# V of later batches by casting DMA, recalibrated plan constants, and q and k of two batches through the DMA crossbar

## The chip, the cores and the metric

One core of a Trainium2 chip runs the whole program. The metric is device microseconds (us) of one execution. The kernel before: 208.59 us, the median of three runs (207.99 to 209.14). "Span" is the time from the first to the last instruction of the profiled execution, some 2 us less than the run time. "Clock" is the mean granted TensorE clock, 1.0 being full. The names of engines are those of the profile: PE (matmul), PEld (weight load), DVE (vector), ACT (scalar), POOL (GpSimd), SP (sync, which only issues DMAs here).

## The reference, cut to what matters

```python
B, H, S, D = 4, 8, 768, 64              # q, k, v: float32, 0.1 * randn
# attention: heads 0, 2, 6 causal over everything; the other five see 4 sink keys and a window of 64
a = softmax(mask(q @ k.T / sqrt(D)));  x = (a @ v) as (B, S, 512)
# wave MLP
theta = x @ w_theta
zr, zi = x * cos(theta), x * sin(theta)
u = x + w_tok_r @ zr + w_tok_i @ zi     # mixes over the 768 tokens
out = u + maximum(u @ w_ch, 0)
```

## The kernel before: the parts that matter here

The kernel doesn't issue instructions in program order. It describes steps, each with the engines that may take it, an assumed duration and the steps it must follow, and a list scheduler fixes, at build time, the order of every engine. At run time each engine works strictly through its list; semaphores only make it wait. Batches are counted 1 to 4 in this text, 0 to 3 in the code.

```python
# q, k: casting loads from the POOL queue, then 12 PE transposes into a PSUM bank, then one copy
# that also puts the tokens in order
def turn_qk(what, b, n):
    pt = state["pt", what, n] = mine_bf()
    for j in range(NB):
        for x, h in enumerate(PAIRS[n]):
            nc.tensor.transpose(pt[64 * x:64 * x + 64, j * 128:(j + 1) * 128], state[what, b][:, h, j * D:(j + 1) * D], ident)

def keep_qk(what, n):
    dst = (qT if what == "q" else kT)[n]
    copy(dst.rearrange("d (p j) -> d p j", j=NB), state.pop(("pt", what, n))[:, :S].rearrange("d (j p) -> d p j", j=NB))

# V: float32 loads from the SP queue, a cast on DVE or POOL, and for the five window heads a copy
# shifted by 64 tokens
def load_v(b, n, after=None): ...
    for x, h in enumerate(PAIRS[n]):
        nc.sync.dma_start(out=t[:, x], in_=src[:, h])
def cast_v(b, n): copy(vt[:, h0:h1 + 1:2, :, :D], state["v", b, n])
def shift_v(b, n, x):
    copy(vx[:64, s], vt[:64, h]); copy(vx[64:, s, 1:], vt[64:, h, :NB - 1])

# x of batches 2 to 4 and most u are already transposed by DMA, from the SP queue
def send_x(b, i): ... nc.sync.dma_start_transpose(...)
# ... (cuts: scores, exponentials, values, theta, waves zr and zi, mix, channel, stores, the scheduler)
```

The softmax here doesn't subtract the row's maximum and nothing guards it: scores larger than these inputs give would overflow.

## Time and profile before

| | before |
|---|---|
| run time, median of 3 | 208.59 us |
| span, clock | 206.3 us, 0.998 |
| PE busy; PE idle | 179.0 us; 27.3 us |
| q of batch 2 lands | 41.3 us |
| values of batch 3 start; theta of batch 4 starts; end | 116.8; 167.4; 206.3 us |

### The profile page before, as it was taken

What the parts mean: (1) busy time and instruction counts of PE and PEld (TensorE: products, weight loads), DVE (VectorE), ACT (ScalarE), POOL (GpSimd) and SP (SyncE); (2) the same over time, 40 slices, a digit from 0 to 9 for tenths busy, and PEclk for the clock granted to TensorE, in tenths of its full rate; (3) what the DMA queues carried; (4) which work ended last, traced back from release to release, by engine and by line L of the source; (5) the groups of instructions that cost most, each with busy time, mean ns of one, the idle gap of its engine ahead of it and who ended that gap; (6) DMA issues with size and microseconds to landing.
All of it is one profiled execution on the core that took longest, in us unless ns stands there. A gap on an engine that the chain in (4) does not pass through costs nothing.

```text
span 206.3 us, 4846 instructions
## 1 busy us (share of the span) xinstructions
PE 179.0 (87%) x1988; PEld 99.4 (48%) x1988; DVE 134.2 (65%) x236; ACT 108.7 (53%) x135; POOL 76.1 (37%) x140
## 2 busy tenths in 40 slices
PE   0689599667999999999999999989699999597992
PEld 0436388444546584454653557534335664242440
DVE  7336966389984574799855287499917446944442
ACT  2397914789885735550677464696683427300010
POOL 8966960394752000674123200099350002900000
PEclk9999999999999999999999999999999999999999
DMA  5998999999999995952223047784223254113404
GB/s 169 182 222 168 157 199 196 192 202 208 206 204 204 115 126 134 232 144 102 54 81 126 4 78 130 185 180 96 49 81 102 79 102 105 55 47 76 153 25 152
DMA packets 58252, 27.45 MB, mean 133 GB/s; under 512 B 44408, under 2 KB 55160, under 8 KB 58232
## 3 DMA queue, kind: packets, MB, share of 16 engines
q1 hardware_dynamic: 47704, 17.85, 40.6%
q0 software_dynamic: 10528, 9.31, 28.3%
q8 instruction: 15, 0.25, 0.6%
q14 instruction: 5, 0.04, 0.1%
HBM read 25.71 MB, written 6.29 MB: 155 GB/s over the span
## 4 chain that ended last, share of the span: by engine, by line
PE 64%; DVE 14%; DMA 13%; ACT 4%; POOL 2%; issue 1%; DVEq 0%; POOLq 0%
PE bank L502 28%; PE bank L525 9%; DMA qb<-in_q_dram 8%; PE pair L366 7%; DVE zr L243 7%; PE pair L453 7%; PE pair L479 6%; PE bank L300 5%; DMA kb<-in_k_dram 3%; DVE zi L243 2%; DVE qT L240 1%; DMA uT<-u 1%; DVE vx L240 1%; PE bank L545 1%; DMA out_dram<-ot 1%
## 5 line engine op out<-in xcount | busy, mean ns | idle before, releaser
L502 PE MATMUL bank<-zr,wtokTr 128*128 128x512 bf16 x144 | 38.6, 380 | 4.3 <-DVE zr L243 3.4
L502 PE MATMUL bank<-zi,wtokTi 128*128 128x512 bf16 x144 | 38.3, 379 | 0.2 <-DVE zi L243 0.2
L366 PE MATMUL pair<-qT,kT 64*64 64x128 bf16 (+5 forms) x380 | 26.7, 262 | 5.1 <-ACT P L385 2.1
L506 DVE TENSOR_TENSOR u<-x,bank 128x512 bf16<-128x512 bf16 x24 | 16.3, 684 | 18.6 <-PE bank L502 18.5
L525 PE MATMUL bank<-w_ch_sb,uT 128*128 128x512 bf16 x96 | 24.1, 380 | 1.9 <-DMA uT<-u 1.5
L247 POOL TENSOR_SCALAR_AFFINE_SELECT P<-P 128x256 bf16<-128x256 bf16 (+1 forms) x48 | 18.2, 398 | 20.1 <-ACT P L385 11.0
L243 POOL TENSOR_TENSOR zi<-x,st 128x512 bf16<-128x512 bf16 x11 | 14.7, 1350 | 29.0 <-ACT st L486 28.9
L529 DVE SCALAR_TENSOR_TENSOR ot<-bank,u 128x512 f32<-128x512 f32 x24 | 16.5, 689 | 13.5 <-PE bank L525 13.2
L243 DVE TENSOR_TENSOR zr<-x,ct 128x512 bf16<-128x512 bf16 x24 | 22.9, 992 | 1.5 <-ACT ct L484 1.5
L366 PEld LDWEIGHTS <-kT 64*64 64x64 bf16 (+1 forms) x380 | 13.0, 111 | 22.4 <-issue 19.5
L385 ACT ACTIVATE P<-pair 128x1024 bf16<-128x1024 f32 (+2 forms) x24 | 21.8, 922 | 3.0 <-PE pair L366 2.8
L479 PE MATMUL pair<-w_theta_sb,xT 128*128 128x512 bf16 x96 | 22.8, 379 | 0.3 <-ACT st L486 0.2
L502 PEld LDWEIGHTS <-wtokTi 128*128 128x128 bf16 x144 | 13.5, 98 | 17.3 <-issue 2.1
L502 PEld LDWEIGHTS <-wtokTr 128*128 128x128 bf16 x144 | 12.6, 98 | 18.9 <-issue 6.5
L382 ACT ACTIVATE P_st<-pair 128x512 bf16<-128x512 f32 (+1 forms) x16 | 12.8, 813 | 12.9 <-PE pair L366 12.8
L240 ACT COPY uT<-bank 128x512 bf16<-128x512 bf16 x5 | 2.9, 585 | 29.3 <-PE bank L515 29.3
L240 POOL CAST vt<-st_v 128x768 bf16<-128x768 f32 x9 | 10.3, 1167 | 20.7 <-DMA st_v<-in_v_dram 20.6
L484 ACT ACTIVATE ct<-pair,half_pi 128x1024 f32<-128x1024 f32 x12 | 13.1, 1118 | 8.0 <-PE pair L479 5.1
L460 DVE TENSOR_TENSOR x<-pair,r 128x512 bf16<-128x512 f32 x24 | 16.6, 691 | 0.8
L453 PE MATMUL pair<-vx,P_st 128*128 128x65 bf16 x120 | 16.0, 200 | 0.3 <-DVE P_st L402 0.3
L300 PE MATMUL bank<-ident,kb 128*64 128x128 bf16 x192 | 8.9, 244 | 8.4 <-DVE kb L240 5.2
L453 PE MATMUL pair<-vt,P_st 128*128 128x65 bf16 x120 | 16.0, 200 | 0.0
(77 smaller groups left out, 291.6 us busy)
## 6 DMA issues: line engine op xcount, KB each, us to landing
st_v<-in_v_dram SPq DMA_DIRECT2D x32, 192.0 KB
out_dram<-ot SPq DMA_DIRECT2D x24, 256.0 KB
qb<-in_q_dram POOLq DMA_DIRECT2D x3, 768.0 KB, 16.8
kb<-in_k_dram POOLq DMA_DIRECT2D x3, 768.0 KB, 19.6
wtok<-in_moe_w_tok_r_dram POOLq DMA_DIRECT2D x3, 384.0 KB, 15.4
wtok<-in_moe_w_tok_i_dram POOLq DMA_DIRECT2D x3, 384.0 KB, 16.6
w_theta_sb<-in_moe_w_theta_dram POOLq DMA_DIRECT2D x1, 512.0 KB, 9.5
w_ch_sb<-in_moe_w_ch_dram POOLq DMA_DIRECT2D x1, 512.0 KB, 24.3
```

The lines of the kernel that those rows point to most:

```text
L240: {"ACT": nc.scalar.copy, "DVE": nc.vector.tensor_copy, "POOL": nc.gpsimd.tensor_copy}[state["step"].eng](o, i)
L243: {"DVE": nc.vector, "POOL": nc.gpsimd}[state["step"].eng].tensor_tensor(o, a, b, ALU.mult)
L247: nc.gpsimd.affine_select(out=t, in_=t, compare_op=ALU.is_ge, fill=0.0, base=base, pattern=pattern, channel_multiplier=cm)
L300: nc.tensor.transpose(pt[64 * x:64 * x + 64, j * 128:(j + 1) * 128], state[what, b][:, h, j * D:(j + 1) * D], ident)
L366: nc.tensor.matmul(ps[half, yy, c:c + w], l, r, start=True, stop=True, skip_group_check=True)
L385: nc.scalar.activation(P.rearrange("p (y c) -> p y c", y=2), ps[:, :, :w0], AF.Exp, scale=scale)
L453: nc.tensor.matmul(o, l, r, start=(m == 0), stop=True, skip_group_check=True)
L460: nc.vector.tensor_tensor(dst, av[:, :, :, :D], r.unsqueeze(3).to_broadcast([128, 2, 4, D]), ALU.mult)
L479: nc.tensor.matmul(ps[:, y], state["xT", b][:, kk, (i + y) * 128:(i + y + 1) * 128], w_theta_sb[:, kk], start=(kk == 0), stop=(kk == KD - 1))
L502: nc.tensor.matmul(py, wtokT[n][:, s, t * 128:(t + 1) * 128], z[:, s], start=(g == 0 and m == 0), stop=(g == 2 and m == 3))
L525: nc.tensor.matmul(pc, uT[:, kk], w_ch_sb[:, kk], start=(kk == 0), stop=(kk == KD - 1))
L529: nc.vector.scalar_tensor_tensor(ot, state.pop(("pc", b, t)), 0.0, state.pop(("u", b, t)), ALU.max, ALU.add)
```

## The change

Its intent is to take work off engines that the end waits for. V of batches 2 to 4 is cast by the DMA that loads it and shifted by four DMA moves in SBUF, so DVE and POOL lose the casts and shifts. q and k of batches 3 and 4 no longer go through PE: DVE puts the two heads of a pair side by side (`qp`), the DMA crossbar transposes, and a copy on DVE, ACT or POOL orders the tokens. The durations that the scheduler assumes are set anew. To make room, q and k have one buffer each instead of two. The core of the diff:

```diff
-                    ns += 0.7 * max(0, min(ns, free[other] - t))
+                    ns += max(0, free[other] - t) if e == "DVE" else 0.3 * max(0, free[other] - t)
@@ buffers (the transposes land in the four wtok buffers)
+        "qp": (8, [128, NB, 2, D], BF16),
         "wtok": (4, [128, 2, S], BF16),
@@ V
+    def fetch_v(b, half):
+        heads = slice(4 * half, 4 * half + 4)
+        nc.gpsimd.dma_start(out=vts[b % 2][:, heads, :, :D], in_=v[b].rearrange("h (j p) d -> p h j d", p=128)[:, heads])
+    def move_v(b):
+        for s, h in ((slice(0, 1), slice(4, 5)), (slice(1, 5), slice(1, 8, 2))):
+            nc.sync.dma_start(out=x[:64, s], in_=t[:64, h])
+            nc.sync.dma_start(out=x[64:, s, 1:], in_=t[64:, h, :NB - 1])
@@ q, k
+    def pair_qk(what, b, n):
+        nc.vector.tensor_copy(t, state[what, b][:, h0:h1 + 1:2].rearrange("p x (j d) -> p j x d", d=D))
+    def send_qk(what, n):
+        nc.sync.dma_start_transpose(t, state.pop(("qp", what, n)).rearrange("p j x d -> p (j x d)"))
@@ turn_steps
+                if b > 1:
+                    pair = paired[what, b, n] = add("DVE", 350, ...pair_qk..., take="qp", port=True)
+                    tp = add("SP", 1250, ...send_qk..., [pair], take="wtok")
+                    land = add("DMAH", 600, None, [tp], give=[pair])
+                    kept[what, b, n] = add({"DVE": 960, "ACT": 1550, "POOL": 1520}, 0, ...keep_qk..., [land] + old, give=[tp], port=True)
+                    continue
@@ assumed durations (the rest alike)
-    gate = [add("DMA", ns, None) for ns in (3500, 6500)]
+    gate = [add("DMA", ns, None) for ns in (6500, 5000)]
-                    shift[b, h] = add({"DVE": 340, "POOL": 960}, ...
+                    shift[b, h] = add({"DVE": 510, "POOL": 1000}, ...
```

More of the change, by code (lines that the diff above doesn't have):

```diff
@@ L204 @@
     kS = [None] + [big.tile([128, 32], BF16, name=f"kS{n}") for n in (1, 2, 3)]
-    vt = big.tile([128, H, NB, D + 1], BF16, name="vt")
-    vx = big.tile([128, len(STREAM), NB, D + 1], BF16, name="vx")
+    vts = [big.tile([128, H, NB, D + 1], BF16, name="vt0")]
+    vxs = [big.tile([128, len(STREAM), NB, D + 1], BF16, name="vx0")]
+    v_room = big.tile([128, 4, 2, NB, D], F32, name="v_room")
+    room = v_room.rearrange("p n x j d -> p (n x j d)").bitcast(BF16)
+    e0, e1 = H * NB * (D + 1), len(STREAM) * NB * (D + 1)
+    vts.append(room[:, :e0].rearrange("p (h j c) -> p h j c", h=H, j=NB))
+    vxs.append(room[:, e0:e0 + e1].rearrange("p (s j c) -> p s j c", s=len(STREAM), j=NB))
     vs = big.tile([128, B, len(STREAM), D + 1], BF16, name="vs")
@@ L223 @@
         "st": (2, [128, 2, DM], F32),
+        "qp": (8, [128, NB, 2, D], BF16),
         "wtok": (4, [128, 2, S], BF16),
-        "st_v": (4, [128, 2, NB, D], F32),
     }
     buffers = {name: [(psum if name in ("pair", "bank") else big).tile(shape, dt, name=f"{name}{i}") for i in range(n)] for name, (n, shape, dt) in SLOTS.items()}
+    SLOTS["st_v"] = (4, None, None)
+    buffers["st_v"] = [v_room[:, n] for n in range(4)]
     state = {}
@@ L251, in load_qk @@
     def load_qk(what, b, heads):
-        if (what, b) not in state:
-            state[what, b] = two.tile([128, H, NB * D], BF16, tag=f"{what}b", name=f"{what}b")
+        state[what, b] = state[what, 0]
         src = {"q": q, "k": k}[what][b].rearrange("h (p j) d -> p h (j d)", p=128)
@@ L263, in cast_first, with load_v, cast_v, shift_v @@
         copy(state[what, 0][:, 0:3:2], state.pop(("first", what)))
-    def load_v(b, n, after=None):
-        src = v[b].rearrange("h (j p) d -> p h j d", p=128)
-        t = state["v", b, n] = mine()
-        if after is not None:
-            nc.vector.tensor_copy(t[:, :, 0, 0], after[:, :2])
+    def load_v(n, after):
+        src = v[0].rearrange("h (j p) d -> p h j d", p=128)
+        t = state["v", n] = mine()
+        nc.vector.tensor_copy(t[:, :, 0, 0], after[:, :2])
         for x, h in enumerate(PAIRS[n]):
             nc.sync.dma_start(out=t[:, x], in_=src[:, h])
-    def cast_v(b, n):
+    def cast_v(n):
         h0, h1 = PAIRS[n]
-        copy(vt[:, h0:h1 + 1:2, :, :D], state["v", b, n])
-    def shift_v(b, n, x):
+        copy(vts[0][:, h0:h1 + 1:2, :, :D], state["v", n])
+    def shift_v(n, x):
         h = PAIRS[n][x]
         s = STREAM.index(h)
-        copy(vx[:64, s], vt[:64, h])
-        copy(vx[64:, s, 1:], vt[64:, h, :NB - 1])
+        copy(vxs[0][:64, s], vts[0][:64, h])
+        copy(vxs[0][64:, s, 1:], vts[0][64:, h, :NB - 1])
+    def ones_v():
+        nc.gpsimd.memset(vts[1][:, :, :, D], 1.0)
+        nc.gpsimd.memset(vxs[1][64:, :, 0], 0.0)
+        nc.gpsimd.memset(vxs[1][64:, :, 0, D], 1.0)
+    def fetch_v(b, half):
+        heads = slice(4 * half, 4 * half + 4)
+        nc.gpsimd.dma_start(out=vts[b % 2][:, heads, :, :D], in_=v[b].rearrange("h (j p) d -> p h j d", p=128)[:, heads])
+    def move_v(b):
+        t, x = vts[b % 2], vxs[b % 2]
+        for s, h in ((slice(0, 1), slice(4, 5)), (slice(1, 5), slice(1, 8, 2))):
+            nc.sync.dma_start(out=x[:64, s], in_=t[:64, h])
+            nc.sync.dma_start(out=x[64:, s, 1:], in_=t[64:, h, :NB - 1])
     def sink_keys(n):
@@ L300, in turn_qk @@
                 nc.tensor.transpose(pt[64 * x:64 * x + 64, j * 128:(j + 1) * 128], state[what, b][:, h, j * D:(j + 1) * D], ident)
+    def pair_qk(what, b, n):
+        h0, h1 = PAIRS[n]
+        t = state["qp", what, n] = mine()
+        nc.vector.tensor_copy(t, state[what, b][:, h0:h1 + 1:2].rearrange("p x (j d) -> p j x d", d=D))
+    def send_qk(what, n):
+        t = mine()[:, 0].rearrange("p (j t) -> p j t", j=NB)
+        state["pt", what, n] = t.rearrange("p j t -> p (j t)")
+        nc.sync.dma_start_transpose(t, state.pop(("qp", what, n)).rearrange("p j x d -> p (j x d)"))
     def keep_qk(what, n):
@@ L437, in values @@
         pav = mine()
+        vt, vx = vts[b % 2], vxs[b % 2]
         state["av", b, i] = av = pav[:, :, :4 * (D + 1)].rearrange("p t (g c) -> p t g c", c=D + 1)
@@ L555 @@
     for what in "qk":
-        state[what, 0] = two.tile([128, H, NB * D], BF16, tag=f"{what}b", name=f"{what}b")
+        state[what, 0] = two.tile([128, H, NB * D], BF16, tag=f"{what}b", name=f"{what}b", bufs=1)
     for heads in (slice(4, 7, 2), slice(1, 8, 2)):
@@ L579, in clear @@
             nc.gpsimd.memset(p_sink, 0.0)
-            nc.gpsimd.memset(vt[:, :, :, D], 1.0)
-            nc.gpsimd.memset(vx[64:, :, 0], 0.0)
-            nc.gpsimd.memset(vx[:, :, :, D], 1.0)
+            nc.gpsimd.memset(vts[0][:, :, :, D], 1.0)
+            nc.gpsimd.memset(vxs[0][64:, :, 0], 0.0)
+            nc.gpsimd.memset(vxs[0][:, :, :, D], 1.0)
         elif n == 2:
@@ L609 @@
         land = add("DMAH", 700, None, [issue])
-        landed[what, 0, 0] = add({"DVE": 460, "ACT": 700} if what == "k" else {"ACT": 700, "DVE": 460}, 0, lambda what=what: cast_first(what), [land], give=[issue], bias=10 ** 6)
+        landed[what, 0, 0] = add({"DVE": 480, "ACT": 750}, 0, lambda what=what: cast_first(what), [land], give=[issue], bias=10 ** 6)
     turned, kept, sinkk, scored, sunk, cast, shift = {}, {}, {}, {}, {}, {}, {}
@@ L614 @@
     weight = {}
+    paired = {}
+    lands_v = {}
     last_pool = []
@@ L638, in turn_steps @@
                         old.append(sinkk[b - 1, n])
-                tp = add("PE", 340, lambda what=what, b=b, n=n: turn_qk(what, b, n), [landed[what, b, n]], take="bank", mode="64c")
-                kept[what, b, n] = add({"DVE": 950, "ACT": 780}, 0, lambda what=what, n=n: keep_qk(what, n), [tp] + old, give=[tp])
+                if b > 1:
+                    pair = paired[what, b, n] = add("DVE", 350, lambda what=what, b=b, n=n: pair_qk(what, b, n), [landed[what, b, n]], take="qp", port=True)
+                    tp = add("SP", 1250, lambda what=what, n=n: send_qk(what, n), [pair], take="wtok")
+                    land = add("DMAH", 600, None, [tp], give=[pair])
+                    kept[what, b, n] = add({"DVE": 960, "ACT": 1550, "POOL": 1520}, 0, lambda what=what, n=n: keep_qk(what, n), [land] + old, give=[tp], port=True)
+                    continue
+                tp = turned[what, b, n] = add("PE", 340, lambda what=what, b=b, n=n: turn_qk(what, b, n), [landed[what, b, n]], take="bank", mode="64c")
+                kept[what, b, n] = add({"DVE": 930, "ACT": 750}, 0, lambda what=what, n=n: keep_qk(what, n), [tp] + old, give=[tp])
             if n:
@@ L644, in v_steps @@
     def v_steps(b):
-        for n in range(4):
-            if b == 0:
-                issue = add("DVE", 200, lambda n=n: load_v(0, n, kT[n // 2]), [kept["k", 0, n // 2]], take="st_v")
+        if b == 0:
+            for n in range(4):
+                issue = add("DVE", 200, lambda n=n: load_v(n, kT[n // 2]), [kept["k", 0, n // 2]], take="st_v")
                 land = add("DMAH", 2000, None, [issue])
-            else:
-                issue = add("SP", 700, lambda b=b, n=n: load_v(b, n), [cast[b - 1, n], xk[b - 1, 5]], take="st_v")
-                land = add("DMAH", 2000, None, [issue])
-            old = [s for key, s in av.items() if key[0] == b - 1] if b else [cleared[1]]
-            cast[b, n] = add({"DVE": 570, "POOL": 830}, 0, lambda b=b, n=n: cast_v(b, n), [land] + old, give=[issue], port=True)
-            for x, h in enumerate(PAIRS[n]):
-                if not IS_RETR[h]:
-                    shift[b, h] = add({"DVE": 340, "POOL": 960}, 0, lambda b=b, n=n, x=x: shift_v(b, n, x), [cast[b, n]] + old, port=True)
+                cast[b, n] = add({"DVE": 570, "POOL": 830}, 0, lambda n=n: cast_v(n), [land, cleared[1]], give=[issue], port=True)
+                for x, h in enumerate(PAIRS[n]):
+                    if not IS_RETR[h]:
+                        shift[b, h] = add({"DVE": 510, "POOL": 1000}, 0, lambda n=n, x=x: shift_v(n, x), [cast[b, n]], port=True)
+            return
+        old = [s for key, s in av.items() if key[0] == b - 2] if b > 1 else list(cast.values())
+        if b == 1:
+            old = [add("POOL", 700, ones_v, old)]
+        lands = []
+        for half in range(2):
+            issue = add("POOL", 900, lambda half=half: fetch_v(b, half), old + last_pool, bias=-20000)
+            last_pool[:] = [issue]
+            lands.append(add("DMA", 3500, None, [issue]))
+        move = add("SP", 1400, lambda: move_v(b), lands)
+        moved = add("DMAH", 500, None, [move])
+        lands_v[b] = lands
+        for h in STREAM:
+            shift[b, h] = moved
     def attention_steps(b):
@@ L671, in attention_steps @@
                 old = [s for key, s in av.items() if key[0] == b - 1] if b else [cleared[1]]
-                se = add("ACT", 600, sink_exps, [sp] + old, give=[sp], mode="exp")
+                se = add("ACT", 690, sink_exps, [sp] + old, give=[sp], mode="exp")
                 sunk[b] = (sp, se)
@@ L688, in attention_steps @@
                 pn = [x for x in range(4) if h in PAIRS[x]][0]
-                need.append(cast[b, pn])
+                need.append(cast[b, pn] if b == 0 else lands_v[b][h // 4])
                 if IS_RETR[h]:
@@ L697, in attention_steps @@
             old = [ud[b - 2, t] for t in range(NB)] if b > 1 else []
-            norm[b, i] = add("DVE", 850, lambda b=b, i=i: normalize(b, i), [av[b, i]] + old, give=[av[b, i]])
+            norm[b, i] = add("DVE", 920, lambda b=b, i=i: normalize(b, i), [av[b, i]] + old, give=[av[b, i]])
             old = [th[b - 1, t, y] for t in (0, 2, 4) for y in range(2)] if b else []
@@ L709, in attention_steps @@
             old = [mixed[b - 2, t, g] for t in range(NB) for g in range(3)] if b > 1 else []
-            c = add("ACT", 930, lambda b=b, i=i: wave(b, i, "ct"), [th[b, i, 0], th[b, i, 1]], take="ct", give=[th[b, i, 0]], mode="sin")
-            s = add("ACT", 930, lambda b=b, i=i: wave(b, i, "st"), [th[b, i, 0], th[b, i, 1], c], take="st", give=[th[b, i, 0]], mode="sin")
+            c = add("ACT", 1000, lambda b=b, i=i: wave(b, i, "ct"), [th[b, i, 0], th[b, i, 1]], take="ct", give=[th[b, i, 0]], mode="sin")
+            s = add("ACT", 1000, lambda b=b, i=i: wave(b, i, "st"), [th[b, i, 0], th[b, i, 1], c], take="st", give=[th[b, i, 0]], mode="sin")
             for y in range(2):
@@ L751, in load_steps @@
                 landed[what, b, n] = land
-    load_steps(1, [])
+    load_steps(1, [turned[what, 0, n] for what in "qk" for n in range(4)])
+    v_steps(1)
     weights(2, 2, [])
@@ L769 @@
         turn_steps(b)
-        v_steps(b)
         if b == 1:
-            sink_steps(1, [sink_done[0], cast[1, 0]])
+            sink_steps(1, [sink_done[0], lands_v[1][0]])
         if b + 1 < B:
-            load_steps(b + 1, [kept[what, b - 1, n] for what in "qk" for n in range(4)])
+            load_steps(b + 1, [(turned if b < 2 else paired)[what, b, n] for what in "qk" for n in range(4)])
+            v_steps(b + 1)
         attention_steps(b)
```

## The prediction

> **What bounds the kernel now.** I read the totals first, then the busy time in stretches of 5 us, then the chain of work that ended last, and only then single instructions.
>
> ```profile
> span 206.3 us, 4846 instructions
> PE 179.0 (87%) x1988; PEld 99.4 (48%) x1988; DVE 134.2 (65%) x236; ACT 108.7 (53%) x135; POOL 76.1 (37%) x140
> PEclk9999999999999999999999999999999999999999
> DMA  5998999999999995952223047784223254113404
> ```
>
> PE is busy for 179.0 of 206.3 us at the full clock, so PE is the bound, and there are 27.3 us of PE idle time. The DMA row says that the first 15 of the 40 slices (77 us) are full of transfers; later they are thin. The 5 us windows say where PE idles:
>
> ```profile
> 40.00:45.00 5.00, 2.68 (x53) 2.02 (x54) 3.03 (x5) 2.85 (x5) 4.87 (x7) 1.00 1.25 199
> 45.00:50.00 5.00, 3.08 (x56) 1.95 (x55) 5.00 (x6) 4.95 (x7) 2.41 (x3) 1.00 1.20 207
> ...
> 110.00:115.00 5.00, 5.00 (x36) 2.14 (x33) 1.34 (x2) 3.61 (x6) 2.86 (x8) 1.00 0.41 131
> 115.00:120.00 5.00, 5.00 (x68) 2.51 (x66) 2.75 (x7) 1.82 (x4) 0.03 (x1) 1.00 0.12 23
> ...
> 145.00:150.00 5.00, 3.31 (x54) 1.58 (x52) 4.25 (x8) 3.90 (x6) 1.49 (x3) 1.00 0.27 52
> ```
>
> After the window come PE, weight loads, DVE, ACT, POOL, clock, DMA share and GB/s. From 60 to 130 us PE has no idle time at all. Idle PE lies at the start (0 to 30 us: 10.9), at 40 to 60 us (5.1), at 130 to 150 us (2.6) and in the last 30 us (about 8.3). Only the two middle ones are touched by this change. The chain tells what PE waits for there, and what PE does at 98 us:
>
> ```profile
> 24.54 16.77 DMA qb<-in_q_dram
> ...
> 44.64 3.13 DVE zr L243 x2
> ...
> 50.65 0.94 DVE vt L240 x2
> ...
> 52.30 0.72 DVE vx L240
> ...
> 98.08 0.79 PE bank L300 x24
> 98.87 0.97 PE bank L502 x4
> 99.84 0.79 PE bank L300 x24
> ```
>
> Columns: start, length, work. At 41.3 us PE gets q of batch 2, a load that took 16.8 us; then the chain runs on DVE until 57.3 us, through products (zr, zi), evictions of qT and kT, and the casts and shifts of V (vt, vx). At 98 us (batch 3) the transposes of q and k are themselves the chain: PE is full and they are part of its work.
>
> **What the Trainium skill says.** "DMA: Bandwidth & Descriptors", section "SWDGE vs HWDGE vs iDMA": a cast in a DMA needs the GpSimd-issued path, a DMA transpose the SP or ACT one. The change obeys this; in the kernel before, the casting loads of q and k already come from POOL and the transposes of x and u from SP. Same page, section "Specifications": pieces under 512 B don't reach line rate. The trace agrees: the first V batch is 6144 pieces of 256 B, some 3390 started in the busiest 5 us, thus about 9 us for 1.57 MB, while a q or k batch of the same bytes in 1024 pieces lands 3.9 to 4.1 us after the one before (68.5 and 72.5 us, when alone). "SBUF — State Buffer", section "SBUF: two separate sides": the port pair that DVE and GpSimd share is an exclusive lock. The trace agrees in kind: a DVE product of 128x512 takes 0.68 us alone, and the four from 133.2 us take 4.43 us together beside POOL's products. "VectorE: DVE Perf Modes", section "The three transpose paths", gives the crossbar 1309 ns for a 128x128 block; here the issue of a 128x512 transpose holds SP 1.2 us, and PE waits 2.4 us for one on the path at 185.8 us.
>
> **The change part by part.** (1) V of batches 2 to 4. Gone are 12 of 16 casts and 30 of 40 shift copies: DVE has 2 casts and 10 shifts left (7 and 32 before), POOL 2 and none (9 and 8 before). By the group rows (DVE cast 0.60, shifts 0.31 and 0.39; POOL cast 1.17, shifts 0.62) this is 5 x 0.60 + 11 x 0.70 = 10.7 us of DVE and 7 x 1.17 + 8 x 0.62 = 13.1 us of POOL. In its place are two casting loads per batch, in pieces of 256 B read and 128 B written, and four small moves in SBUF. I estimate 9 us of transfer per batch, as for the 256-byte pieces above. The loads of batch 2's V leave the SP queue, where 4 pairs of them ran beside the weights and q from 18.5 us on; now they stand in the POOL queue behind q and k of batch 2. So q no longer shares its 16.8 us with them: I estimate that it lands 4 to 7 us sooner. The second and third sets of token weights and the channel weights come after V, some 4 us later than now relative to k; they were not on the chain.
>
> (2) q and k of batches 3 and 4. PE loses 192 of 384 transposes (its instruction list is 384 rows shorter: a load and a matmul each). In the chain batch 3's 96 cost 0.79 + 0.79 + 0.46 + 1.13 = 3.17 us, about 33 ns each; two mix groups beside them take 0.97 instead of 0.86, so 3.4 us in all, in a stretch with no PE idle. Of batch 4's 96, 36 (1.4 us) lie on the chain and the other 60 (2.0 us) fall at 131 to 136 us, where PE has holes anyway; I count 0.5. Sum: 5.3 us. Added: 16 pair copies on DVE, which I estimate at 0.35 us (5.6 us), from the shift copies' 0.31 us for half the columns; 16 SP transposes of 128x768, 1.2 us or so each; and 16 copies back, now from SBUF, split over DVE 5, ACT 4, POOL 7. The evictions from PSUM fall from 12 to 8 on DVE (0.96 each) and 20 to 8 on ACT (0.80). DVE: plus 5.6 + 4.8, minus 3.8, against the 10.7 saved by V: some 4 us less work than before. POOL takes some 10 us and had 13 freed. No engine becomes the bound.
>
> (3) Recalibration and single buffers. The order of the last batch's tail, from theta to the last store (167.6 us on, 38.7 us), is nearly the same list on every engine; I count 0. q and k of a later batch now load only after the former was read, but at 77 us and later the DMA row shows room.
>
> (4) The middle idle stretches. At 41 to 57 us DVE loses the vt and vx work, 0.94 + 2.26 = 3.2 us on the chain, and q comes sooner; of 5.1 us of PE idle I count 3.5 back. At 130 to 150 us DVE loses a qT copy (0.96) and 2.62 us of shifts plus 0.84 of cast; of 2.6 us of PE idle I count 1.5.
>
> (5) Losses: a new chain load, pair copy, transpose, copy back, and a longer SP queue in which a waiting move holds up stores and transposes. I put in 1.0 us.
>
> Sum: 5.3 + 3.5 + 1.5 - 1.0 = 9.3 us off 208.6: 199.3 us.
>
> **The rivals.** (a) V becomes the late one. If a 128-byte casting write costs double, V of batch 2 takes 18 us instead of 9 and holds back all behind it in the queue: token weights, q and k of batch 3. Against it: values of batch 2 start only at 65.6 us, and with q landing at about 35 us and k 4 us later V would be there by 57 us even so. For it: the pair copies of batch 3 stand on DVE before the last two normalizations of batch 2, so a late q there stalls DVE and, behind it, PE. Then (4) shrinks to about 1 and 3 us are lost: 205 us. (b) The DVE to SP to landing to copy-back chain is late for batches 3 and 4, so PE waits where the transposes were. Against it: the pair copies stand in batch 2's values, some 25 us ahead of the scores of batch 3. For it: one in-order SP queue with 50 transposes, with the V moves (which wait for the load) between them. It would give back 3 to 4 us: 203 us. (c) The time freed is hidden anyway: ACT is busy 4.3 to 5.0 of each 5 us in 45 to 60 us, so ACT may set that stage with its waves and exponentials, and only the PE part remains: 202 us. (d) The gain is larger, if q's early landing pulls all of batch 2 ahead and fills the idle at 20 to 30 us too: 195 us.
>
> **Range and chances.** PE's saved transposes are the firmest part, since they lie in a stretch without PE idle. With them alone I get 203 to 204; with everything, 195. I predict 199.3 us, 195.0 to 204.5 in 8 of 10. Faster by over 2% means under 204.4: 0.80; within 2%: 0.16; slower: 0.04.
>
> **What would show it.** PE busy time should be 172 to 173 us and PE idle 22 to 24. q of batch 2 should land before 38 us, and the chain at 40 to 57 us should no longer hold vt or vx; no PE transposes should stand near 98 or 122 us. A PE wait of over 2 us for qT, kT, a V load or the token weights after 60 us would prove (a) or (b). Wrong altogether if casting V takes over 20 us a batch or the SP queue holds the stores so that PE's banks fill.

## More of the kernel before

The totals, the clock row and the chain are shown in the prediction. What it doesn't show is the middle of the kernel by stretches of 5 us. The columns after the stretch are its length, then busy time (and instructions) of PE, PEld, DVE, ACT and POOL, the clock, the mean number of busy DMA engines as a share, and GB/s:

```profile
85.00:90.00 5.00, 5.00 (x28) 2.41 (x27) 3.63 (x6) 2.16 (x3) 4.24 (x4) 1.00 1.17 215
90.00:95.00 5.00, 5.00 (x28) 2.39 (x27) 4.78 (x7) 0.83 (x2) 4.61 (x5) 1.00 0.19 73
95.00:100.00 5.00, 5.00 (x51) 2.41 (x50) 4.09 (x12) 0.80 (x1) 0.45 (x2) 1.00 0.37 112
105.00:110.00 5.00, 5.00 (x39) 1.99 (x39) 3.07 (x6) 3.59 (x5) 0.29 (x1) 1.00 0.18 61
```

PE never idles here and the clock is full. The same stretches of the changed kernel follow below.

## The result, and the profile after

The changed kernel took **218.86 us** (median of 4 runs, 217.26 to 222.03) against 208.87 (207.99 to 213.27) for the kernel before in the same rounds: ratio 1.047, 95% interval 1.036 to 1.057. It is slower, and outside the predicted range. Here and below a ratio is fast runs of one kernel against fast runs of the kernel before in the same rounds, so it isn't quite the ratio of the medians.

The page of the changed kernel, in the same four lines as the prediction showed of before:

```profile
span 215.4 us, 4465 instructions
PE 177.4 (82%) x1796; PEld 93.9 (44%) x1796; DVE 125.7 (58%) x220; ACT 109.6 (51%) x131; POOL 87.9 (41%) x145
PEclk9999999996999999995879999999999999999999
DMA  5996999999999949999965676652031463313413
```

PE has 192 transposes fewer (1796 rows against 1988) and yet is busy nearly as long, 177.4 us. It idles 38.0 us, 10.7 more than before; 1.6 us less busy and 10.7 more idle make the 9.1 us by which the span grew. The clock row, all 9 before, has 6, 5, 8 and 7 in it. The DMA row is full in slices 16 to 20 (81 to 108 us), where the row of before reads 5, 9, 5, 2, 2, 2 from 77 to 108 us. The windows say the same:

```profile
40.00:45.00 5.00, 3.16 (x47) 1.80 (x45) 5.00 (x3) 3.08 (x4) 4.74 (x5) 1.00 2.46 175
45.00:50.00 5.00, 2.72 (x21) 1.34 (x21) 4.98 (x8) 4.56 (x6) 2.55 (x7) 0.86 1.18 207
...
85.00:90.00 5.00, 2.63 (x13) 0.98 (x10) 2.33 (x4) 0.00 (x0) 0.58 (x1) 1.00 1.29 191
90.00:95.00 5.00, 2.12 (x12) 0.93 (x12) 2.68 (x5) 0.79 (x1) 3.26 (x3) 1.00 1.47 171
95.00:100.00 5.00, 1.85 (x6) 0.75 (x7) 1.29 (x2) 4.58 (x5) 1.81 (x2) 0.64 1.89 169
...
105.00:110.00 5.00, 2.87 (x7) 1.02 (x7) 3.01 (x6) 4.22 (x4) 4.70 (x9) 0.66 0.56 202
```

From 85 to 100 us PE works 6.6 of 15 us where it worked all 15, while DVE, ACT and POOL work only 5.4 to 6.3 us each. No engine is the bound; all of them wait. The chain (start, length, work) names what for:

```profile
37.79 2.68 DVE qT L248 x3
40.47 4.85 DVE zr L251 x2
...
79.39 16.63 DMA wtok<-qp x2
...
97.51 0.58 ACT uT L248
...
100.65 5.64 DMA out_dram<-ot
...
106.39 0.70 DVE ot L563
...
107.13 7.62 PE bank L536 x28
```

`wtok<-qp` is a crossbar transpose of q or k. Where the chain of before had PE matmuls without a break from 60 to 130 us, here two transposes stand for 16.63 us, and then a plain store for 5.64. The waits from 78 to 112 us (who waited, for what: us in all, times, longest):

```profile
POOL qT L248 <- DMA wtok<-qp: 25.1, 3, 15.0
DVE kT L248 <- DMA wtok<-qp: 13.9, 2, 7.9
ACT qT L248 <- DMA wtok<-qp: 10.4, 1, 10.4
DVE ot L563 <- DMA out_dram<-ot: 6.9, 2, 6.2
PE bank L559 <- ACT uT L248: 5.1, 1, 5.1
PE bank L549 <- DVE u L540: 3.3, 1, 3.3
PE bank L536 <- DVE ot L563: 2.7, 1, 2.7
```

The copies after the transposes stand in order on three engines, and behind them stand the waves, products and copies that PE needs: PE's own longest wait is put down to "ACT uT", a copy of 0.58 us which had been standing behind a copy of qT that waited 10.4 us and a copy of kT. PE never waits for qT or kT themselves in this stretch: what it lacks is older work (uT, u, ot) that stands behind batch 3's copies.

By milestones (us), the loss sits in one place:

| start of | before | after | change in this stage |
|---|---|---|---|
| theta of batch 2 | 75.7 | 75.2 | -0.5 |
| values of batch 3 | 116.8 | 124.3 | +8.0 |
| values of batch 4 | 156.2 | 165.8 | +2.1 |
| end | 206.3 | 215.4 | -0.5 |

How long does a transpose take? The trace gives for every DMA its issue and the moment at which the last of its 16 engines reported. It stands in no page; I list it for SP's transposes of interest in the two kernels. Batch 3 has an eighth, the first, issued at 73.3 us before these loads began; it landed after 4.0.

| DMA | issued at (us) | lands after (us) |
|---|---|---|
| after: q, k of batch 3 | 79.4, 80.7, 82.5, 86.8, 89.8, 95.7, 97.2 | 8.2, 11.0, 11.6, 9.2, 8.8, 8.6, 8.5 |
| after: q, k of batch 4 | 109.3, 110.8, 117.3, 118.6, 125.2, 127.4, 131.3, 132.7 | 2.8, 2.8, 2.8, 2.8, 3.2, 2.8, 2.8, 4.3 |
| after: x, u, nothing beside them | 115 to 140 | 2.4 |
| before: x of batch 2 | 67.4, 68.8 | 7.1, 6.2 |

In the changed kernel the loads of q, k and V of batch 4 were issued at 78.9 to 82.0 us from the POOL queue and landed at 88.0, 92.9, 99.0 and 105.4 us: exactly while batch 3's transposes were slow. They suffer as well: batch 3's own V halves, which had landed 3.1 and 3.0 us after the load ahead of them, have become 6.1 and 6.4 us apart in batch 4 (3.1 and 4.2 in pe_turns below, which has no transposes of q or k). The last row is the sobering one. The kernel before already showed a transpose of 7.1 us, at 67.4 us, while the load of k for batch 4 ran until 72.5 us. It was in the trace when I predicted, and I had only looked at durations of issue and at a quiet transpose.

### The profile page after: what moved, and what is told of

It reads as the page before. It is cut to its first block, busy times and chain, and to the rows that moved or that the text cites. A ratio compares the mean times of both kernels' runs of the same rounds, so it can differ in the third digit from the quotient of the medians.

```text
span 215.4 us, 4465 instructions
## 1 busy us (share of the span) xinstructions
PE 177.4 (82%) x1796; PEld 93.9 (44%) x1796; DVE 125.7 (58%) x220; ACT 109.6 (51%) x131; POOL 87.9 (41%) x145
## 2 busy tenths in 40 slices
DMA packets 72875, 29.59 MB, mean 137 GB/s; under 512 B 57112, under 2 KB 69784, under 8 KB 72856
## 4 chain that ended last, share of the span: by engine, by line
PE 60%; DMA 18%; DVE 8%; ACT 6%; issue 3%; POOL 2%; SPq 1%; ACTq 0%; DVEq 0%; POOLq 0%
PE bank L536 28%; PE pair L487 9%; DMA wtok<-qp 8%; PE pair L399 7%; PE bank L559 6%; PE pair L513 5%; DMA out_dram<-ot 5%; DMA kb<-in_k_dram 3%; DVE zr L251 3%; DMA uT<-u 2%; PE bank L322 2%; DVE ot L563 2%; DVE qT L248 2%; PE bank L579 2%; ACT ct L518 1%
## 5 line engine op out<-in xcount | busy, mean ns | idle before, releaser
L536 PE MATMUL bank<-zr,wtokTr 128*128 128x512 bf16 x144 | 40.2, 396 | 4.0 <-DVE ot L563 2.7
L536 PE MATMUL bank<-zi,wtokTi 128*128 128x512 bf16 x144 | 39.8, 394 | 0.0
L399 PE MATMUL pair<-qT,kT 64*64 64x128 bf16 (+6 forms) x380 | 27.0, 267 | 6.6 <-ACT P L418 2.2
L559 PE MATMUL bank<-w_ch_sb,uT 128*128 128x512 bf16 x96 | 25.3, 392 | 8.4 <-ACT uT L248 5.5
L251 POOL TENSOR_TENSOR zi<-x,st 128x512 bf16<-128x512 bf16 x15 | 19.3, 1312 | 29.9 <-DVE zr L251 21.9
L255 POOL TENSOR_SCALAR_AFFINE_SELECT P<-P 128x256 bf16<-128x256 bf16 (+1 forms) x48 | 17.8, 392 | 22.6 <-ACT P L423 13.3
L415 ACT ACTIVATE P_st<-pair 128x1024 bf16<-128x1024 f32 (+1 forms) x16 | 12.6, 813 | 15.6 <-PE pair L399 15.6
L248 POOL COPY qT<-wtok 128x768 bf16<-128x768 bf16 x5 | 7.8, 1578 | 27.8 <-DMA wtok<-qp 25.1
L435 DVE TENSOR_TENSOR P_st<-P_st,m_stream 128x512 bf16<-128x512 bf16 (+2 forms) x24 | 13.7, 580 | 7.6 <-ACT P_st L426 5.3
L559 PEld LDWEIGHTS <-uT 128*128 128x128 bf16 x96 | 8.3, 99 | 19.8 <-ACT uT L248 6.2
L513 PEld LDWEIGHTS <-xT 128*128 128x128 bf16 x96 | 9.1, 98 | 12.5 <-issue 1.7
```

What stands on the lines that cost most here:

```text
L251: {"DVE": nc.vector, "POOL": nc.gpsimd}[state["step"].eng].tensor_tensor(o, a, b, ALU.mult)
L255: nc.gpsimd.affine_select(out=t, in_=t, compare_op=ALU.is_ge, fill=0.0, base=base, pattern=pattern, channel_multiplier=cm)
L399: nc.tensor.matmul(ps[half, yy, c:c + w], l, r, start=True, stop=True, skip_group_check=True)
L513: nc.tensor.matmul(ps[:, y], state["xT", b][:, kk, (i + y) * 128:(i + y + 1) * 128], w_theta_sb[:, kk], start=(kk == 0), stop=(kk == KD - 1))
L536: nc.tensor.matmul(py, wtokT[n][:, s, t * 128:(t + 1) * 128], z[:, s], start=(g == 0 and m == 0), stop=(g == 2 and m == 3))
L559: nc.tensor.matmul(pc, uT[:, kk], w_ch_sb[:, kk], start=(kk == 0), stop=(kk == KD - 1))
```

## The experiments

**Theory A**: crossbar transposes that run beside casting loads land three to four times later, and the in-order copies behind them pass that on to PE. **Rivals**: B, the recalibrated order loses the time; C, the crossbar route loses by its own work (copies on DVE, ACT, POOL, the longer SP queue), contention or not; V by DMA is to blame.

All variants are of the changed kernel or the kernel before, with small edits. All were found correct against the reference. A run counts as slow when it is over 1.5% above the fastest of its kernel. "Old plan" means the plan constants of the kernel before.

**1. pe_turns: q and k of all batches on PE again, the rest as changed.**

```diff
-                if b > 1:
+                if b > 9:
                     pair = paired[what, b, n] = ...
```

> The changed kernel with q and k of batches 3 and 4 turned by PE again; V by DMA and the recalibrated plan stay. Theory A (the crossbar transposes of batch 3 collide with the loads of batch 4 between 79 and 105 us, and everything behind the copies back stalls): about 204 to 209 us, no PE gap over 2 us between 75 and 110 us, no half clock there. Rival B (V by DMA and the new order are what costs): stays at 213 us or more. Rival C (the crossbar chain is too long by itself): the same number as A here, told apart by late_loads.

Measured: 210.4 us (208.76 to 214.27), ratio 1.013 (1.001 to 1.026). Without the crossbar 3.3 of the 4.7% are gone, and PE is busy where it stood:

```profile
90.00:95.00 5.00, 4.95 (x24) 2.29 (x24) 2.75 (x5) 0.00 (x0) 0.00 (x0) 1.00 0.37 135
```

Between 75 and 110 us PE has no gap over 1.4 us and no half clock, as A said; the time is 1.4 us above A's range. The crossbar is the greater part, but 1.3% (0.1 to 2.6) stay lost with V by DMA and the recalibrated plan, which I hadn't expected. The variant moves something else too: the loads of batch 4 now wait for PE's transposes of batch 3 and are issued at 102.4 us, not 78.9. So this run alone doesn't separate the crossbar from the date of the loads; plain_moves (8), whose loads are issued at 78.6 us, does.

**2. xbar_only: the kernel before with the crossbar and the recalibrated plan; V loaded, cast and shifted as before.**

> The kernel before with the recalibrated plan and q, k of batches 3 and 4 through the crossbar; V stays on the SP loads, casts and shifts. Theory A: q and k of batch 4 still load beside the transposes of batch 3, though V of batch 4 does not: 211 to 217 us, transposes 5 us or more from issue to landing. Rival B: about 205 us, since V is not touched. Rival C: 214 to 218 us.

Measured: 219.75 us (217.86 to 222.13), ratio 1.055 (1.042 to 1.069). This is above the range of every theory, so it is a miss for all three. It doesn't clear V by DMA either, for another loss stands in this run:

```profile
50.00:55.00 5.00, 0.57 (x3) 0.17 (x2) 0.00 (x0) 0.00 (x0) 2.48 (x4) 0.93 0.67 131
55.00:60.00 5.00, 0.00 (x0) 0.00 (x0) 0.00 (x0) 0.88 (x1) 4.80 (x10) 0.50 0.76 91
```

PE idles for 9.6 us from 50.6 us on, behind the float32 load of V for batch 2, and the first transpose of q or k is issued only at 72.5 us. The next run shows that stop without a crossbar. That V by DMA isn't the cause rests on vdma_oldplan and xbar_only_oldplan (6 and 7).

**3. recal_only: the kernel before with the new plan constants only.**

> The kernel before with nothing but the recalibrated plan constants. Theory A and rival C: 206 to 211 us, within 1.5% of before. Rival B in the form that the plan itself is worse: 212 us or more.

Measured: 222.91 us (219.72 to 223.32), ratio 1.066 (1.044 to 1.088). For A and C a clear miss, of 12 us; it is what B foresaw for the plan alone. Its profiled run was slow (0.2% above a run that counts as fast, at the same clock of 0.944), so I take from it only where it stops, which is where xbar_only stops too:

```profile
37.18 23.18 DMA st_v<-in_v_dram
60.36 0.02 issue
```

The float32 load of V for batch 2, in the SP queue, takes 23.2 us, and in the new order its cast stands on POOL ahead of POOL's share of the products, so PE stands still from 52.6 to 66.7 us. The new constants were made for a kernel without these loads. My reading, not shown by a run of its own, is that an order fixed at build time is only as good as the landing times it assumes.

**4. late_loads: as changed, but the loads of batch 4 wait (by two tiny POOL copies that read qT and kT and write into the load's buffers) until batch 3's copies back are done.**

```diff
+            if b == 2:
+                held = add("POOL", 150, lambda: hold_load(), [kept[what, b, n] for what in "qk" for n in range(4)])
+                load_steps(b + 1, [held])
```

> The changed kernel, but q, k and V of batch 4 are loaded only after the transposed q and k of batch 3 have been copied back (two tiny POOL copies hold the loads). Theory A: transposes of batch 3 land in 2.8 us like those of batch 4 do, the PE gaps at 87 to 107 us go, 207 to 212 us. Rival C (in-order SP queue, four landing buffers, copies back): still 215 us or more, with the gaps in their place.

Measured: 215.71 us (214.33 to 216.45), ratio 1.038 (1.029 to 1.048). As a time this is a miss for A and inside C's range. The trace says why: batch 3's transposes now land in 2.7 to 3.7 us (the first, issued at 73.4 us, in 4.3, as it took 4.0 before), near what A says, but the loads moved to 99 to 128 us, and there they lie beside three transposes of u (8.5 to 9.4 us) and five of batch 4's own q and k (7.0 to 10.6 us). The chain:

```profile
102.94 9.37 DMA uT<-u
...
116.55 9.40 DMA wtok<-qp
```

I had removed one collision and made another.

**5. xbar_b4 and xbar_b3: the crossbar for one batch only.**

```diff
-                if b > 1:
+                if b > 2:        # xbar_b4;  "if b == 2:" in xbar_b3
```

> The changed kernel with only batch 4's q and k through the crossbar; batch 3's turned by PE. No loads of a later batch run beside batch 4's transposes. Theory A: transposes land in about 2.8 us and the time is no worse than pe_turns: 207 to 211 us. Rival C (the chain itself is too long wherever it stands): 213 us or more.

> The mirror: only batch 3's q and k through the crossbar, beside the loads of batch 4. Theory A: all of the loss is here, 215 to 220 us, transposes 8 us and more. Rival C: half of the loss, about 213 us.

Measured: xbar_b4 214.48 us (212.59 to 216.21), ratio 1.026 (1.018 to 1.034); xbar_b3 224.88 us (223.13 to 226.94), ratio 1.071 (1.061 to 1.080). Both missed A's numbers; xbar_b4 fell into C's range, xbar_b3 above both. In xbar_b4 batch 4's transposes were to run alone, and did not: V of batch 4, issued at 104.9 and 106.2 us, lands at 128 and 134 us, and the transposes issued from 112.7 to 127.2 take 7.4 to 11.0 us; after 135 us they take 2.8. In xbar_b3 (slow, so only a pointer) seven of batch 3's take 6.9 to 13.3 us, beside loads that land from 90 to 109 us. In each run the slow transposes are those that meet casting loads, wherever they lie. Why batch 3 alone by crossbar costs more than both batches is not settled: its profile has one idle stretch of PE of 7.9 us, and after 90 us the clock is halved for 23.9 us in all, against 10.2 in the changed kernel. That was a slow run, though its fast runs have clocks of 0.904 and 0.920 as well.

**6. vdma_oldplan and after_oldplan: the plan constants of the kernel before, with V by DMA alone, and with the whole rest of the change.**

> V of batches 2 to 4 by DMA alone, PE turns q and k of all batches, and the constants of the plan as they were before. Theory A with the addition that the recalibrated order has a price of its own: 203 to 208 us, below pe_turns (210.4). Rival B in its stronger form (V by DMA itself costs, by its 128-byte writes and single q, k buffers): 209 us or more.

> The changed kernel with the constants of the plan as they were. If the loss is the crossbar's collision with the loads, it stays at 213 to 220 us; if the recalibrated order is what loses, it falls to 205 to 210 us.

Measured: vdma_oldplan **206.05 us** (205.27 to 207.19), ratio 0.990 (0.982 to 0.998), the best version found, by 1.0%, which is clear of noise; after_oldplan 216.7 us (215.79 to 217.96), ratio 1.040 (1.033 to 1.047). Both are as A expected. Under the old plan, too, the crossbar costs 5%: rival B falls as the main cause of the whole change's loss, and V by DMA is no loss by itself.

**7. xbar_only_oldplan: the kernel before with the crossbar alone.**

> The kernel before with the crossbar alone: old plan constants, V loaded on SP, cast and shifted by engines as before. If the crossbar loses by itself, as the pairs with V by DMA say (+4 to +5%): 215 to 221 us. If it needs V's casting loads from the GpSimd queue to lose: 206 to 211 us.

Measured: 217.29 us (216.75 to 223.42), ratio 1.042 (1.032 to 1.052); the profiled run was slow. As expected if the crossbar loses by itself. That the casting loads of q and k are enough for it is the reading of a slow profile: the transposes issued at 84.5 and 87.7 us, beside batch 4's loads of q and k, took 10.0 and 10.1 us.

With this the three parts are measured in all eight combinations (the single buffers of q and k come with V by DMA and with the crossbar, and have no run of their own). Loss against the kernel before, in per cent of its time (95% intervals of 0.7 to 1.3 either way, 2.2 for the 6.6):

| | old plan, V as before | old plan, V by DMA | new plan, V as before | new plan, V by DMA |
|---|---|---|---|---|
| q, k on PE | 0 | -1.0 | +6.6 | +1.3 |
| q, k of batches 3, 4 by crossbar | +4.2 | +4.0 | +5.5 | +4.7 |

So the parts don't add. The crossbar costs 4.2, 5.0 and 3.3% in three columns, but nothing can be read in the third, where the new plan alone has already lost as much.

**8. plain_moves: the sixteen transposes become plain moves of the same bytes, in the same queue and order.** Its q and k of batches 3 and 4 are scrambled. (Scores of such inputs are about 0.01 in size, so the weights are nearly uniform whatever q and k are. It is no kernel to use.)

```diff
-        nc.sync.dma_start_transpose(t, state.pop(("qp", what, n)).rearrange("p j x d -> p (j x d)"))
+        nc.sync.dma_start(out=t.rearrange("p j t -> p (j t)"), in_=state.pop(("qp", what, n)).rearrange("p j x d -> p (j x d)"))
```

> The sixteen DMA transposes of q and k of batches 3 and 4 become plain moves of the same bytes in SBUF, in the same queue and place (so q and k of these batches are wrong, on purpose). Theory A (it is the transposing that suffers beside casting loads): the plain moves land in under 4 us beside the loads of batch 4 and the time falls to 207 to 212 us. Rival A2 (any move in the SP queue waits for the engines that the loads fill; that it transposes does not matter): the moves of batch 3 take 6 us or more, and the time stays at 215 to 219.

Measured: 208.46 us (207.92 to 211.76), ratio 0.999 (0.990 to 1.009); the profiled run was slow (span 209.9), so the landings below are a pointer; the time is from fast runs. The time is that of the first expectation, the landing nearly that of the second. Beside the loads a plain move takes 4.7 to 7.7 us, in place of 8.2 to 11.6 for a transpose; in quiet 2.2 in place of 2.8. So the other DMAs of the SP queue are late beside these loads too, as the store of 5.64 us in the chain above was, but the transpose takes half again as long, and it holds the SP queue for 1.2 to 4.1 us at its issue where a move beside the loads holds it for 0.5 to 0.8. Which of the two costs more, the landing or the hold, no run separates. The last transpose of batch 3 landed at 105.7 us, the last move at 95.9. The waits from 78 to 112 us shrink accordingly:

```profile
POOL qT L248 <- DMA wtok<-qp: 18.9, 3, 15.1
DVE kT L248 <- DMA wtok<-qp: 4.2, 1, 4.2
ACT qT L248 <- DMA wtok<-qp: 3.8, 1, 3.8
```

This run also answers C. All else of the crossbar route is in it, the pair copies, the copies back, the waits on buffers, the PE work saved; and it is no slower than PE's transposes under the same plan (0.999 against 1.013, intervals that overlap). Whether the route would have gained something, as the 4.3 us predicted net for it say, if a transpose were as quick as a move, is within the noise and not shown.

What differs between the two in the trace is packets. First the changed kernel, then plain_moves:

```profile
DMA packets 72875, 29.59 MB, mean 137 GB/s; under 512 B 57112, under 2 KB 69784, under 8 KB 72856
```

```profile
DMA packets 62379, 29.59 MB, mean 141 GB/s; under 512 B 44568, under 2 KB 59288, under 8 KB 62360
```

The bytes are the same. Per transfer, plain_moves has (57112 - 44568) / 16 = 784 fewer packets under 512 B and 784 - (72875 - 62379) / 16 = 128 more larger ones. The sizes of single records in the traces say what they are: a transpose is 768 of 256 B and 32 of 4 B (800, as pe_turns with its 44312 under 512 B confirms), a move 128 of 1536 B and 16 of 4 B. The Trainium skill, "DMA: Bandwidth & Descriptors", section "Queues, rings and completion order", says that a DMA engine takes turns between the queues that have work for it, a packet at a time. If the records of the trace are such packets, a transfer with six times as many data packets needs more turns beside a busy queue than a move of the same bytes. The landings agree in direction; that this is the mechanism is argued, not shown, for the same section lets a packet hold several pieces of data, the trace doesn't say how they are packed, and no run varied the packets alone.

**9. no_overlap and no_overlap_oldplan: late_loads, with batch 4's loads in the order V, k, q, so that its transposes cannot start before the rest has landed.**

```diff
+                last_pool[:] = [held]
+                v_steps(b + 1)
+                load_steps(b + 1, [held], "kq")
```

> As late_loads, with the loads of batch 4 held until batch 3's copies back are done, and in the order V, k, q, so that batch 4's transposes cannot start before all its loads have landed: no transpose of q or k lies beside a load. Theory A (the overlap is the whole loss): all sixteen transposes land in under 4 us and the time is 207 to 212 us, near the 210.4 of the version without crossbar. Rival C (the copies back and the in-order queue cost as much by themselves): 214 us or more although the transposes are quick. Rival D (the hold makes batch 4 late): PE waits over 3 us for batch 4's q, 213 to 217.

> The same with the plan constants of the kernel before, to stand against V by DMA under the old constants (206.05) and the whole change under them (216.7). Theory A: 204 to 210 us. Rivals C and D: 212 us or more.

Measured: no_overlap 211.87 us (211.1 to 216.48), ratio 1.015 (1.006 to 1.025): a hit for A in time, and within the intervals the same as without crossbar (1.013), though not all sixteen transposes land in under 4 us. Of batch 3's transposes the first lands in 4.1, the others in 2.7 to 3.7 us. Batch 4's first three take 4.5 to 5.7 us, the last five 2.8. But the price of the order is on its chain:

```profile
104.13 21.29 DMA qb<-in_q_dram
...
127.01 4.81 DMA wtok<-qp
```

q of batch 4, last of four loads, lands 21.3 us after its issue; the loads still lie beside the transposes of u, which take 5.2 to 11.6 us. So rival D has a share in what remains. no_overlap_oldplan: 212.03 us (209.8 to 213.65), ratio 1.009 (0.996 to 1.022); two of its four runs, the profiled one among them, were slow; of its fast runs 209.80 is inside A's range and 210.77 between the two expectations. Against vdma_oldplan (0.990) it still loses about 2%, so even with the overlap mostly gone the crossbar doesn't pay. How much of these 2% is the hold, and how much the queue, is open.

## Why the prediction was wrong, by its own steps

*Part (2), PE's saved transposes: right in kind, useless in the sum.* PE has the 192 fewer. At 33 ns each its busy time should have come to 179.0 - 6.3 = 172.7 us, as predicted; the profile has 177.4. Work at half clock accounts for the 4.7 us of difference: the granted clock is 0.5 at 48.6 us for 3.41 us, at 96.4 for 6.83 and at 106.6 for 3.41, and PE is busy for 11.4 us of these 13.7, which at full clock would be 5.7 us less (an estimate, if every instruction takes double). The mean matmul of the mix rows went from 380 to 396 ns. The Trainium skill, "TensorE: Matmul & The Clock Gate", section "Part 1: The HAM clock gate (the "warmup" mystery)", has a half rate after an idle window of about 3.4 us. The trace agrees in the rate and the window: the three starts lie 14 and 3 steps of 3.41 us apart. It doesn't agree that the window must be idle throughout: in the 3.41 us before the three starts PE idled for 2.1, 3.3 and 2.2 us. Nor is a gap's length enough: 3.3 us at 87.6 us, spread over two such windows (1.9 and 1.4), and 3.4 us at 44.4 us in pe_turns were followed by no half clock. The prediction counted idle PE at its face value; such gaps can cost more.

*Part (5), the losses, and rival (b): this is the step that failed. The cost of a transpose was read in quiet, and the overlap with the next batch's loads was left out.* I put in 1.0 us for "a new chain load, pair copy, transpose, copy back, and a longer SP queue", gave 3 to 4 us to rival (b), and took the quiet transpose (1.2 us of issue, 2.4 us on the path) as the cost; beside the loads it was 8.2 to 11.6 us. The steps through the table of eight, in us of 208.6: V by DMA -1.0% or 2.0 us gained; the crossbar on top of it from 0.990 to 1.040, 10.4 us lost; the new constants on top of both from 1.040 to 1.047, 1.4 us lost, which is within the noise. They add up to +9.7 us because each starts where the last ended; another order gives other shares. Predicted for the crossbar was -5.3 + 1.0 = -4.3 us. The argument against (b), that the pair copies stand 25 us ahead of the scores, holds at the head of the line only: the first pair copy is at 71.8 us, but seven of eight transposes were issued from 79 to 97 us, through one SP queue and four `wtok` buffers that each wait for a copy back, and beside the loads of batch 4. "At 77 us and later the DMA row shows room" was true of before, where q and k of batch 4 had been issued at 52.0 and 53.0 us and had landed by 72.5; it was this change that moved them to 78.9 us, behind the reading of the one buffer, and V after them into the same queue. That the transposes are the cause of most of the loss is shown by pe_turns and plain_moves together, and under the old plan by vdma_oldplan against after_oldplan; that the collision with the loads makes them slow, by late_loads, no_overlap and xbar_b4, where the slow ones move with the loads; that the single buffers set the date of the loads is read from the diff and the order, and no run tried two.

*Parts (1) and (4), V: the mechanism was right and the size too large.* A casting half of V lands 3.0 to 3.1 us after the load ahead of it, thus some 6 us a batch and not 9 (12.5 for batch 4, beside the transposes); rival (a) is false. q of batch 2 landed at 35.3 us, 6 sooner than before, as predicted (4 to 7). vt and vx are gone from the chain of 40 to 57 us. But of 3.5 and 1.5 us only 2.0 in all were measured (vdma_oldplan). In the changed kernel theta of batch 2 starts 0.5 us earlier, not 3.5: with the new constants two zr products stand for 4.85 us of the chain at 40.5 us beside POOL's zi (one of them takes 4.33 us, where 0.68 is usual), kT's copy stands behind, and PE idles from 43.8 to 47.3 us, just before the first half clock.

*Part (3), the recalibration, counted 0: wrong.* Looking at the tail alone missed it. It costs +1.3 - (-1.0) = 2.3% with V by DMA, 6.6% alone, and 0.7% (within the noise) with all parts.

*Rivals (c) and (d)* needed a gain and had none. The sign that the prediction named for (b), a wait of PE of over 2 us for qT or kT, did not come: after 60 us PE's single waits of over 2 us are for uT (5.1), u (3.3) and ot (2.7). (b) came true by another path. POOL, DVE and ACT waited for the landings, 15.0, 7.9 and 10.4 us at the longest, and PE starved of the older work that stood behind them in order; two transposes stand for 16.63 us of the chain. I had looked for the wait on the wrong engine.

## What to carry to other kernels

Ask of a DMA that is to stand on the critical path not how long it takes alone, but how long it takes in the window in which it will run, and look in the trace for one of its kind that ran beside the same traffic: here it was there, 7.1 us instead of 2.4. Moving work from a busy engine to a DMA also moves a wait onto every engine that stands, in order, behind the landing, and idle PE can be paid twice, through the clock. Look for the wait on the engine that stands before the landing; the engine that starves may name something else. Try the parts of a combined change one by one: only one of the three didn't lose, and it gained 1%.

## What the Trainium skill lacked or had wrong

- "Advanced Engine Details and Errata", section "X-Bar Transpose (TRN2)", says that transpose DMAs are as fast as regular ones (and, two lines on, about 90% of a copy's bandwidth). Of the same 192 KB a transpose of 128x768 in SBUF landed after 2.8 us and a plain move after 2.2 us in quiet, and after 8.2 to 11.6 against 4.7 to 7.7 us beside casting loads.
- "DMA: Bandwidth & Descriptors", section "Rules for kernel authors", says that a transpose beside ordinary DMAs needs nothing. Every run here passed the comparison, so nothing speaks against it for results. The page also has all DMAs share their engines, but how much it costs (transposes 2.8 to 11.6 us, V loads 3.0 to 6.4 us apart) stands on no page that I found.
- No page that I found counts the packets of a transpose (one names a tile of 256 B): the trace has 768 of 256 B and 32 of 4 B for 128x768 of two bytes, where a move has 128 of 1536 B and 16 of 4 B.
- "TensorE: Matmul & The Clock Gate", section "Part 1: The HAM clock gate (the "warmup" mystery)", asks for an idle window before the half rate. Here windows of 3.41 us in which PE idled for only 2.1 and 2.2 us were followed by it.
- "DMA: Bandwidth & Descriptors", section "Specifications", has the limit of 512 B for pieces but not what a casting load in pieces of 256 B read and 128 B written costs: 3.0 to 3.1 us per half batch, 6.1 per batch of V, against 3.9 to 4.1 us for the same bytes of q or k in large pieces.
- No page that I found gives the copy that puts 768 tokens in order within SBUF, 128x768 in bf16: 0.82 us on DVE, 1.50 on ACT, 1.51 on POOL.
